# Filling products of identity and mask in any free bank of PSUM, in front of every operation of TensorE

## The chip, the cores and the metric

One core of one Trainium2 chip runs the kernel. Its engines are TensorE (PE, with its weight loads PEld), VectorE (DVE), ScalarE (ACT), GpSimd (POOL) and SyncE (SP, which here only issues DMAs). The metric is the device time of one execution in microseconds; of several runs the median is given.

## The reference

Attention with decay and without softmax (8 batches, 8 heads, 576 positions, 64 wide), then a mixture of experts with two of eight experts for each of 4608 tokens:

```python
scores = scale * np.matmul(q, k.transpose(0, 1, 3, 2))
Dmat = np.where(rel >= 0, gamma[:, None, None] ** rel[None, :, :], 0.0)
x = np.matmul(scores * Dmat[None], v)            # then (4608, 512)
noisy_logits = x @ w_gate + np.log1p(np.exp(x @ w_noise)) * noise
top2 = np.argpartition(-noisy_logits, 2, axis=1)[:, :2]
...
h = np.maximum(x[mask] @ w1[e], 0.0)             # 512 -> 1024
out[mask] += top2_w[mask, k, None] * (h @ w2[e]) # 1024 -> 512
```

## The kernel before

The attention is worked off in 16 units (a batch of a pair of batches and half of the heads, `u`), each with transposes of k and q (L558, L552), scores (L583), states (L616) and outputs (L651, L661). After each four units, which are one pair of batches, come a tail of 64 positions (L697 to L732), the routing logits (L769), the ranks of tokens (L832, L834), a table of places (L883) and the transposes of rows (L910) that are written to a table in HBM (`xd`). From that table the experts' tokens are gathered (L1026), transposed on TensorE (L1048) or by DMA, and go through the up products (L1103, or L1129 for the wide tiles) and the down products (L1191). Experts' tiles of the first three pairs of batches are worked off between units of attention; the rest follows.

What order the instructions have on each engine is decided when the program is built. All operations are recorded with a cost and a priority in a `Plan`; `Plan.run` then takes, one after another, the operation with the earliest planned start, reserves buffers for it, and keeps a planned clock for each engine (`free`). PSUM is a class "ps" of eight banks in `self.slots["ps"]`; an entry holds the planned time at which the bank comes free, its present user or `None`, and the tile. A bank has a user from the operation that opens it (which has it in `allocs`) until its last reader.

TensorE gets filling products: `warm` (L294) multiplies the identity with 256 columns of the attention's mask and writes the product, which nobody reads, to a bank. At L195 to L197 the planner notes how many of them go in front of an operation: only if that operation is on TensorE, has a planned start before `WARM` (170 us) and opens a bank. The count is 0.8 of the planned gap between the moment when TensorE and the operation's own bank are both free and its start, less 0.2 us, in products of 0.11 us. At L244 to L247, when all is planned, the operations are issued in their order, each behind its fillings. The planned times do not know of the fillings.

Which semaphores an instruction waits for follows from what it reads and writes: a filling that writes a bank waits until the bank's last reader is done, and on TensorE all that stands behind it waits with it.

Of the kernel before, what the change touches and what calls it, by code (L numbers as in the profile page):

```python
# [17 lines left out]
P = 128  # L18
# [36 lines left out]
class Plan:  # L55
# [23 lines left out]
    def op(self, eng, cost, fn, r=(), w=(), prio=0.0, dma=0, after=(), port=False, pace=0.0, slack=0.0, hold=0.0, late=0.0):  # L79
        o = Op()  # L80
        o.i, o.fn, o.prio, o.dma, o.port, o.pace, o.slack, o.hold = len(self.ops), fn, prio, dma, port, pace, slack, hold
        o.late, o.fill = late, 0
        o.eng = eng if isinstance(eng, dict) else {eng: cost}
        o.succ, o.allocs, o.bufs = [], [], []
        preds = set(after)
        for items, wr in ((r, False), (w, True)):
            for it in items:
                b, sub = it if isinstance(it, tuple) else (it, None)
                for s2, o2, w2 in b.acc:
                    if (wr or w2) and (sub is None or s2 is None or s2 == sub):  # L90
                        preds.add(o2)
                if b not in o.bufs:
                    o.bufs.append(b)
        for items, wr in ((r, False), (w, True)):
            for it in items:
                b, sub = it if isinstance(it, tuple) else (it, None)
                if wr:
                    b.acc = [a for a in b.acc if a[1] is o or not (sub is None or a[0] == sub)]
                b.acc.append((sub, o, wr))
        preds.discard(o)  # L100
        for b in o.bufs:
            if b.cls is not None:
                if not b.ops:
                    o.allocs.append(b)
                    self.fifo.setdefault((b.cls, b.stream), []).append(b)
                b.ops.append(o)
                b.left += 1
        o.preds, o.need = preds, len(preds)
        for p in preds:
            p.succ.append(o)  # L110
        self.ops.append(o)
        return o

    def run(self):
        free, dma_free, port, paced = {}, {}, [0.0], 0.0
# [34 lines left out]
        while ready:  # L150
            pick = None
            for o in ready:
                taken = []
                ok = all(b.cls is None or b.t is not None or b in o.allocs for b in o.bufs)
                if not ok:
                    continue
                for n, b in enumerate(o.allocs):
                    k = (b.cls, b.stream)
                    q = self.fifo[k]
                    m = len([t for t in taken if (t[1].cls, t[1].stream) == k])  # L160
                    if q[head[k] + m] is not b:
                        ok = False
                        break
                    x = slot(b, taken)
                    if x is None:
                        ok = False
                        break
                    taken.append((x, b))
                if not ok:
                    continue  # L170
                t0 = max([y[0] for x, b in taken for y in x], default=0.0)
                if o.pace:
                    t0 = max(t0, paced + o.pace)
                best = None
                for e, c in o.eng.items():
                    t = max(t0, free.get(e, 0.0))
                    if o.port and e in ("DVE", "POOL"):
                        t = max(t, port[0])
                    if o.dma and len(lanes[e]) >= 8:
                        t = max(t, lanes[e][-8].fin)  # L180
                    for p in o.preds:
                        t = max(t, p.fin + (o.hold + self.LAT if p.dma else 0.0 if p.on == e else self.LAT + o.late))
                    x = t + c + (self.BIAS.get(e, 0.0) if len(o.eng) > 1 else 0.0)
                    if best is None or x < best[0]:
                        best = x, e, t, c
                _, e, t, c = best
                key = (round(t * 20), o.prio, o.i)
                if pick is None or key < pick[0]:
                    pick = (key, o, e, t, c, taken)
            if pick is None:  # L190
                raise RuntimeError("no operation can go on: " + str([(o.i, o.prio) for o in ready[:20]]))
            _, o, e, t, c, taken = pick
            ready.remove(o)
            o.on = e
            if e == "PE" and t < self.WARM and o.allocs:  # L195
                x = max([free.get(e, 2.5)] + [y[0] for x, b in taken for y in x])
                o.fill = max(0, int((t - x - 0.2) * 0.8 / 0.11))  # L197
            free[e] = t + c
            if o.pace:
                paced = t  # L200
            if o.port and e in ("DVE", "POOL"):
                port[0] = t + c
            o.fin = t + c
            if o.dma:
                x = max(dma_free.get(e, 0.0), t + c)
                if e == "SP":
                    x += o.dma / 0.95
                else:
                    x += o.dma / 0.85
                    if dma_free.get("SP", 0.0) > t + c:  # L210
                        dma_free["SP"] += o.dma

                        for y in lanes["SP"][-8:] if o.dma > 2 else ():
                            if y.fin > t + c + self.DMA_LAT:
                                y.fin += o.dma
                dma_free[e] = x
                o.fin = dma_free[e] + self.DMA_LAT + o.slack
                lanes[e].append(o)
            for x, b in taken:
                for y in x:  # L220
                    y[1] = b
                b.t = x[0][2] if b.n == 1 else x[0][3]
                k = (b.cls, b.stream)
                head[k] += 1
                used[k] = used.get(k, 0) + b.n
            for b in o.bufs:
                if b.cls is None:
                    continue
                b.left -= 1
                if not b.left:  # L230
                    for x in self.slots[b.cls]:
                        if x[1] is b:
                            x[1] = None

                            x[0] = max(p.fin + (self.LAND if p.dma else 0.0) for p in b.ops) + self.LAT
                    used[(b.cls, b.stream)] -= b.n
            for s in o.succ:
                s.need -= 1
                if not s.need:
                    ready.append(s)  # L240
            order.append((o, t))
        assert len(order) == len(self.ops)
        self.log = [(t, o.on, o.fin, o.prio) for o, t in order]
        for o, t in order:  # L244
            if o.fill:
                self.warm([b for b in o.allocs if b.cls == "ps"][0], o.fill)
            o.fn(o.on)  # L247


class Kernel:  # L250
# [40 lines left out]
        else:  # L291
            self.eng(e).tensor_copy(out, in_)  # L292

    def warm(self, b, n):  # L294

        ident, mask = self.fixed["ident"].t, self.fixed["mask"].t
        for _ in range(n):
            self.nc.tensor.matmul(b.t[:, :2 * P], lhsT=ident, rhs=mask.rearrange("p r x -> p (r x)"), start=True, stop=True,  # L298
                                  skip_group_check=True)

    def psum(self, stream, n=1):
# [440 lines left out]
    def route(self, bp, prio):  # L742
# [56 lines left out]
        for j, op in ((0, Alu.max), (1, Alu.min)):  # L799
            o("DVE", DV, lambda e, j=j, op=op: V.tensor_tensor(kw(j), w1(), w2.t, op), ww, [at(("kw", j))])  # L800
# [12 lines left out]
        def s2(out, a, b, op, r, w):  # L813
            o("DVE", DV, lambda e: V.tensor_tensor(out(), a(), b(), op), r, w)
# [674 lines left out]
```

## Time and profile before

| | |
|---|---|
| time, median of 3 runs | 439.73 us (438.94 to 443.84) |
| the profiled execution | 438.11 us, span 436.6 us |
| TensorE busy | 386.1 us, 88% of the span, 4419 products |
| ScalarE, GpSimd, VectorE busy | 263.5, 288.1 and 154.4 us |
| mean granted clock of TensorE | 0.977 |
| moved by DMA | 95.92 MB, 220 GB/s in the mean |

A row of the profile's groups reads: line, engine, operation, what it writes and reads with buffer numbers left out, shapes and count; then busy time and mean ns of one; then the idle time of the engine ahead of these instructions, and what ended it. A row of the timeline has its start, the busy time, and in brackets the idle time ahead of it with what ended it; "issue" there means that the profile shows nothing that it waited for. A row of the stretches has busy times by engine, the clock that TensorE was granted (1.00 is full), the busy share of the DMA engines and GB/s.

### The profile page before, as it was taken

How to read it: one execution, taken by the hardware profiler on the slowest of the kernel's cores; microseconds unless marked ns; L12 is line 12 of the kernel's file. 1: busy time of each engine (PE TensorE's matmuls, PEld its weight loads, DVE VectorE, ACT ScalarE, POOL GpSimd, SP SyncE). 2: the span in 40 equal slices, each digit the busy share in tenths (PEclk: the TensorE clock that was granted, in tenths of full speed). 3: DMA queues.
4: the chain of work that ended last, by engine and by line, in shares of the span. 5: the costliest groups of instructions: out<-in, count | busy, mean ns of one | idle time of the engine just before them, and what ended most of it. 6: DMA issues, size and time to landing. Idle time of an engine off the chain costs nothing. (4 is left out here: it accounts for less than half of the span.)

```text
span 436.6 us, 11260 instructions
## 1 busy us (share of the span) xinstructions
PE 386.1 (88%) x4419; PEld 244.1 (56%) x4419; DVE 154.4 (35%) x455; ACT 263.5 (60%) x462; POOL 288.1 (66%) x315
## 2 busy tenths in 40 slices
PE   4987787876778999968999999999999999999992
PEld 3876576764566666725456654454454454454451
DVE  5654398696419979201034511103202100000001
ACT  2598687883668756433765755736647755555550
POOL 8755684681488836645367777776866878785583
PEclk9999698999899999989999999999999999999998
DMA  7996998999978999923249978999999969879395
GB/s 232 311 282 140 294 284 245 323 270 240 254 229 151 248 227 280 379 84 113 79 140 363 390 184 254 224 292 235 246 246 280 274 123 152 167 116 147 61 122 105
DMA packets 105177, 95.92 MB, mean 220 GB/s; under 512 B 42015, under 2 KB 82464, under 8 KB 105122
## 3 DMA queue, kind: packets, MB, share of 16 engines
q1 hardware_dynamic: 87298, 59.33, 48.4%
q0 software_dynamic: 17824, 35.85, 39.8%
q8 instruction: 35, 0.57, 0.6%
q14 instruction: 20, 0.16, 0.1%
HBM read 72.71 MB, written 26.36 MB: 227 GB/s over the span
## 5 line engine op out<-in xcount | busy, mean ns | idle before, releaser
L1191 PE MATMUL ps<-W,half 128*128 128x512 bf16 x576 | 189.7, 384 | 10.1 <-ACT half L1112 6.6
L1129 PE MATMUL ps<-big,W 128*128 128x512 bf16 (+4 forms) x640 | 182.4, 329 | 0.0
L1112 ACT ACTIVATE half<-ps 128x512 bf16<-128x512 f32 (+5 forms) x190 | 92.0, 503 | 102.3 <-PE ps L1129 59.4
L1235 POOL DMA_INDIRECT out_dram<-half,xg x74 | 96.9, 1309 | 51.6 <-issue 14.1
L1026 POOL DMA_INDIRECT xg<-xd,xi x80 | 82.8, 1036 | 50.0 <-issue 19.7
L1191 PEld LDWEIGHTS <-half 128*128 128x128 bf16 x576 | 55.0, 99 | 73.6 <-ACT half L1112 10.6
L1129 PEld LDWEIGHTS <-W 128*128 128x128 bf16 x640 | 62.5, 98 | 47.2 <-issue 1.0
L1229 ACT ACTIVATE half<-ps,xg 128x512 f32<-128x512 f32 (+1 forms) x57 | 38.5, 676 | 13.8 <-PE ps L1191 11.1
L591 DVE TENSOR_TENSOR half<-ps,mask 128x512 bf16<-128x512 f32 x64 | 40.3, 683 | 16.9 <-PE ps L583 12.8
L290 ACT ACTIVATE half<-ps 128x1024 bf16<-128x1024 bf16 (+1 forms) x38 | 37.0, 998 | 13.3 <-PE ps L558 6.0
L1231 DVE TENSOR_SCALAR half<-ps,xg 64x256 f32<-64x256 f32 (+1 forms) x22 | 13.2, 602 | 89.5 <-PE ps L1201 54.4
L1103 PE MATMUL ps<-half,W 128*128 128x256 bf16 (+1 forms) x288 | 29.3, 255 | 2.1 <-DMA W<-in_moe_w_dram 1.4
L298 PE MATMUL ps<-mask,ident__61 128*128 128x256 bf16 x147 | 21.9, 296 | 6.2 <-POOL mask L361 5.9
L1103 PEld LDWEIGHTS <-W 128*128 128x128 bf16 x288 | 23.9, 98 | 5.8 <-DMA W<-in_moe_w_dram 1.7
L292 DVE CAST W<-big 128x1024 bf16<-128x1024 f32 x18 | 12.0, 709 | 41.9 <-PE ps L1129 20.9
L290 ACT ACTIVATE tb<-ps 64x512 bf16<-64x512 f32 x32 | 18.8, 589 | 8.1 <-PE ps L616 3.7
L290 ACT ACTIVATE W<-big 128x1024 bf16<-128x1024 f32 x22 | 22.7, 1053 | 0.7 <-issue 0.5
L290 ACT ACTIVATE xT<-ps 128x512 bf16<-128x512 f32 (+1 forms) x39 | 19.6, 555 | 4.6 <-PE ps L661 1.8
L616 PE MATMUL ps<-half,half 64*64 64x64 bf16 (+2 forms) x512 | 18.2, 216 | 3.2 <-DVE half L591 1.4
L536 POOL TENSOR_TENSOR half<-big,tab 128x512 bf16<-128x512 f32 x16 | 16.6, 1050 | 5.8 <-DMA big<-in_v_dram 5.8
L529 POOL TENSOR_TENSOR half<-W,tabq 128x1024 bf16<-128x1024 f32 x6 | 11.4, 1901 | 13.1 <-DMA W<-in_q_dram 4.9
L298 PEld LDWEIGHTS <-ident__61 128*128 128x128 bf16 x147 | 14.5, 105 | 8.8 <-POOL ident__61 L353 4.6
(181 smaller groups left out, 436.5 us busy)
## 6 DMA issues: line engine op xcount, KB each, us to landing
big<-in_moe_w_dram SPq DMA_DIRECT2D x40, 512.0 KB
W<-in_moe_w_dram POOLq DMA_DIRECT2D x12, 512.0 KB
xd<-xg SPq DMA_DIRECT2D x16, 264.0 KB
W<-in_q_dram SPq DMA_DIRECT2D x16, 256.0 KB
big<-in_k_dram SPq DMA_DIRECT2D x8, 512.0 KB
big<-in_v_dram SPq DMA_DIRECT2D x8, 512.0 KB
big<-in_q_dram SPq DMA_DIRECT2D x16, 256.0 KB
W<-in_k_dram SPq DMA_DIRECT2D x6, 512.0 KB
```

The lines of the kernel that those rows point to most:

```text
L290: self.nc.scalar.activation(out, in_, Act.Copy)
L298: self.nc.tensor.matmul(b.t[:, :2 * P], lhsT=ident, rhs=mask.rearrange("p r x -> p (r x)"), start=True, stop=True, skip_group_check=True)
L536: self.eng(e).tensor_tensor(o, i, t, Alu.mult)
L591: nc.vector.tensor_tensor(S.t.bitcast(BF16).rearrange("p (h c x) -> p h c x", h=2, c=2)[:, h], p[h].t.rearrange("p (c x) -> p c x", c=2), ...
L616: nc.tensor.matmul(o[h * HD:(h + 1) * HD, hp, n, :], lhsT=kk[:k, r, c, y], rhs=vv[:k, r, c, y].unsqueeze(1).to_broadcast([k, n.stop - n.st ...
L1026: ins = nc.gpsimd.indirect_dma_start(out=x.t[:n, :], out_offset=None, in_=self.xd[:rows, :], in_offset=IOff(ap=xi.t[:n, h:h + 1], axis=0), ...
L1103: nc.tensor.matmul(pv()[:, f2, :], lhsT=w.t[:, o:o + P], rhs=xv()[:, di, :n], start=(di == 0), stop=(di == KD - 1))
L1112: self.nc.scalar.activation(o, i, Act.Relu)
L1129: self.mm = nc.tensor.matmul(p.t[:, :n], lhsT=w.t[:, o:o + P], rhs=xv()[:, di, :n], start=(di == 0), stop=(di == KD - 1))
L1191: self.mm = self.nc.tensor.matmul(po.t, lhsT=hv[:, c:c + P], rhs=self.W[e].t[:, o:o + DM], start=(f == 0), stop=(f == KF - 1))
L1229: nc.scalar.activation(y.t[:n, c], x, Act.Copy, scale=g()[:n])
L1235: ins = nc.gpsimd.indirect_dma_start(out=self.out[:, :], out_offset=IOff(ap=ix()[:n], axis=0), in_=y.t[:n, :], in_offset=None, bounds_chec ...
```

## The change

Fillings are now looked at for every operation of TensorE with a planned start before 170 us, whether it opens a bank or not. They go into the bank without a user that came free earliest, which may or may not be the one that the operation opens. The count comes from the planned gap between TensorE's and that bank's coming free and the operation's start. An operation carries the bank and the count (`o.fill`), and `warm` takes the bank's tile.

```diff
-        o.late, o.fill = late, 0
+        o.late, o.fill = late, None
...
-            if e == "PE" and t < self.WARM and o.allocs:
-                x = max([free.get(e, 2.5)] + [y[0] for x, b in taken for y in x])
-                o.fill = max(0, int((t - x - 0.2) * 0.8 / 0.11))
+            if e == "PE" and t < self.WARM:
+                b = min((x for x in self.slots["ps"] if x[1] is None), key=lambda x: x[0], default=None)
+                n = b and int((t - max(free.get(e, 2.5), b[0]) - 0.2) * 0.8 / 0.11)
+                if n and n > 0:
+                    o.fill = b[2], n
...
             if o.fill:
-                self.warm([b for b in o.allocs if b.cls == "ps"][0], o.fill)
+                self.warm(*o.fill)
...
-    def warm(self, b, n):
+    def warm(self, t, n):
...
-            self.nc.tensor.matmul(b.t[:, :2 * P], lhsT=ident, rhs=mask.rearrange("p r x -> p (r x)"), start=True, stop=True,
+            self.nc.tensor.matmul(t[:, :2 * P], lhsT=ident, rhs=mask[:, :2].rearrange("p r x -> p (r x)"), start=True, stop=True,
```

The mask's tile has two rows of 128, so `mask[:, :2]` is all of it. Two lines more stand in the new kernel from L200 on: L298 of before is L300 now, L651 is L653, and so on.

On TensorE, before, at the end of a unit's states (L616) and the start of the outputs of the unit ahead of it (L651), which the profile has at 74.0 us; `ps4_129` is bank 4 of PSUM, `half` are buffers in SBUF, and the brackets name the engine whose semaphore the row waits for:

```order
L616 LDWEIGHTS half16_98
L616 MATMUL ps0_125<-half19_101,half16_98 64x64
L651 LDWEIGHTS half1_83
L651 MATMUL ps4_129<-half13_95,half1_83 64x8x16 [waits Activation_49]
L651 LDWEIGHTS half1_83
L651 MATMUL ps1_126<-half13_95,half1_83 64x8x16 [waits Activation_49]
```

The same place on TensorE now:

```order
L618 LDWEIGHTS half16_98
L618 MATMUL ps0_125<-half19_101,half16_98 64x64
L300 LDWEIGHTS ident__61
L300 MATMUL ps4_129<-mask_143,ident__61 128x256 [waits Activation_49]
L300 LDWEIGHTS ident__61
L300 MATMUL ps4_129<-mask_143,ident__61 128x256
L300 LDWEIGHTS ident__61
L300 MATMUL ps4_129<-mask_143,ident__61 128x256
L653 LDWEIGHTS half1_83
L653 MATMUL ps4_129<-half13_95,half1_83 64x8x16
L653 LDWEIGHTS half1_83
L653 MATMUL ps1_126<-half13_95,half1_83 64x8x16 [waits Activation_49]
```

Three fillings stand in front of the outputs, in the bank that these open themselves, and the wait for ScalarE has moved from the first output product to the first filling.

On TensorE, before, between two gathered tiles of an expert (the two halves of the buffer `xg5`) that are transposed into one bank, at 86.8 us in the profile (`DMASW1` is the semaphore of the second tile's gather):

```order
L1048 LDWEIGHTS xg5_115
L1048 MATMUL ps0_125<-ident__61,xg5_115 128x128
L1048 LDWEIGHTS xg5_115 [waits DMASW1_49]
L1048 MATMUL ps0_125<-ident__61,xg5_115 128x128
L1048 LDWEIGHTS xg5_115
```

There now:

```order
L1050 LDWEIGHTS xg5_115
L1050 MATMUL ps0_125<-ident__61,xg5_115 128x128
L300 LDWEIGHTS ident__61
L300 MATMUL ps1_126<-mask_143,ident__61 128x256 [waits DVE_49]
L300 LDWEIGHTS ident__61
L300 MATMUL ps1_126<-mask_143,ident__61 128x256
L1050 LDWEIGHTS xg5_115 [waits DMASW1_49]
L1050 MATMUL ps0_125<-ident__61,xg5_115 128x128
```

Two fillings stand between the tiles, in another bank than that of the transposes, and the first of them waits for VectorE, which empties that bank.

## The prediction

> **What bounds the kernel now.** The page comes first: the span, and the row of its costliest groups that holds the filling products (mean in ns behind the busy time, then idle time before them).
>
> ```profile
> span 436.6 us, 11260 instructions
> L298 PE MATMUL ps<-mask,ident__61 128*128 128x256 bf16 x147 | 21.9, 296 | 6.2 <-POOL mask L361 5.9
> q8 instruction: 35, 0.57, 0.6%
> ```
>
> 147 products without a use take 21.9 us of TensorE. Whether time of TensorE is worth anything depends on the stage, so the second view is busy time by stretches: length, then busy us with counts for PE, PEld, DVE, ACT and POOL, granted clock, DMA share, GB/s.
>
> ```profile
> 40.00:80.00 40.00, 31.02 (x736) 26.70 (x737) 25.22 (x66) 29.01 (x48) 25.66 (x27) 0.87 0.95 269
> 80.00:120.00 40.00, 30.00 (x634) 23.85 (x631) 27.84 (x69) 26.60 (x45) 19.46 (x25) 0.96 1.05 267
> 120.00:160.00 40.00, 34.49 (x713) 26.97 (x711) 26.36 (x72) 29.96 (x52) 30.74 (x34) 1.00 0.95 214
> 212.00:430.00 218.00, 215.62 (x1288) 112.61 (x1285) 33.69 (x72) 125.92 (x231) 155.20 (x128) 1.00 0.90 207
> ```
>
> From 212 us on TensorE is busy 215.62 of 218 us at full clock: there it is the bound, and no filling stands there, before or now. In the attention stage, up to 160 us, it is busy 75 to 86% of each stretch, no engine is full, and the DMA share is 0.95 to 1.05: TensorE stands idle some 9 us of every 40 and waits for others, and the inputs arrive at the rate of the DMA. All that the change adds falls between 40 and 125 us, into this stage.
>
> The third view is the granted clock. The first dip in the trace begins at 47.56 us; stretches of 3.41 us laid from there show it whole or not at all (length, PE busy, clock, DMA share, GB/s).
>
> ```profile
> 44.15:47.56 3.41, 1.62 (x36) 1.00 0.99 282
> 47.56:50.97 3.41, 3.27 (x74) 0.50 1.07 320
> 50.97:54.39 3.42, 2.97 (x23) 0.50 1.09 308
> 68.04:71.46 3.42, 0.90 (x9) 1.00 0.80 210
> 71.46:74.87 3.41, 3.28 (x96) 0.50 0.92 259
> 105.59:109.00 3.41, 2.09 (x34) 1.00 0.85 236
> 109.00:112.42 3.42, 3.07 (x107) 1.00 0.70 190
> 112.42:115.83 3.41, 1.41 (x22) 1.00 0.94 256
> 115.83:119.24 3.41, 3.22 (x44) 0.50 1.05 296
> ```
>
> After a stretch with 1.62, 0.90 or 1.41 us of work the clock was 0.50; after one with 2.09 us it stayed 1.00. So in this run the line lies between 1.62 and 2.09 us of work in 3.41 us, and the fillings of before didn't keep TensorE above it at three places.
>
> **The change part by part.** The rule now looks at every operation of TensorE whose planned start is before 170 us, not only at those that open a bank, and puts the fillings into the free bank that came free first. The planned starts don't depend on fillings, so nothing else moves: the rows of DVE, ACT, POOL and SP stand as they stood, waits included, and the diff's slice of the mask is the same 256 columns. On TensorE, 20 groups with 147 products become 27 groups with 172. Seven groups are new, of 2, 5, 3, 2, 4, 3 and 5 products (24 in all); one group grows by one; one of four goes into another bank and loses a wait for ACT that ended nothing, since no idle time stood before it.
>
> Price of one product, from two groups of the old ones on the timeline (start, busy, idle before):
>
> ```profile
> 50.93 1.25 PE L298 MATMUL ps<-mask,ident__61 128*128 128x256 bf16 x5
> 83.76 1.05 PE L298 MATMUL ps<-mask,ident__61 128*128 128x256 bf16 x8
> ```
>
> Eight at full clock take 1.05 us, 0.13 each; five in the slow stretch 1.25, 0.25 each. All 25 are so worth 3.3 us at full clock and 6.3 at half. What counts is what stands behind each group. Here are the old rows around seven of the eight places, in order of time; in brackets the idle time before the row and what ended it.
>
> ```profile
> 40.86 0.55 PE L769 MATMUL ps<-wgn,xT 128*128 128x16 bf16 x16
> 42.14 0.32 PE L710 MATMUL ps<-half 64*64 64x64 bf16 x16 [0.26 <-ACT half L290]
> 45.94 0.62 PE L552 MATMUL ps<-ident__61,half 128*128 128x128 bf16 x8 [2.71 <-POOL half L529]
> 59.39 0.21 PE L651 MATMUL ps<-half,half 64*64 64x128 bf16 x1
> 60.24 0.64 PE L651 MATMUL ps<-half,half 64*64 64x128 bf16 x31 [0.63 <-DVE pay L814]
> 62.60 0.64 PE L583 MATMUL ps<-half,half 64*64 64x128 bf16 x32 [0.28 <-ACT half L290]
> 86.55 0.61 PE L1048 MATMUL ps<-ident__61,xg 128*128 128x128 bf16 x8
> 88.89 0.22 PE L832 MATMUL ps<-MM,ltri 128*128 128x144 bf16 x1 [1.73 <-DVE MM L805]
> 106.91 1.02 PE L1191 MATMUL ps<-W,half 128*128 128x512 bf16 x4 [2.13 <-DMA W<-in_moe_w_dram]
> 119.25 0.55 PE L769 MATMUL ps<-wgn,xT 128*128 128x16 bf16 x16
> 122.64 0.62 PE L697 MATMUL ps<-ident__61,half 128*128 128x128 bf16 x8 [1.06 <-POOL half L688]
> 124.38 0.32 PE L710 MATMUL ps<-half 64*64 64x64 bf16 x16 [0.67 <-ACT half L290]
> ```
>
> - Two in front of the routing logits (L769) at 40.9 us: 0.26 us. The next wait, 0.26 us for ACT's copy, ends when L697's result, which comes before the fillings, has been copied; so they use that wait up. Were they longer, 2.71 us for POOL stand behind. Cost 0.
> - Five in front of the first L651 at 59.4: 0.65 us against 0.63 us of waiting for DVE one product later. Cost 0.0.
> - One more in the group at 61.6: 0.13 against 0.28. Cost 0.
> - Two between the two gathered tiles that L1048 transposes at 86.8: 0.26 against 1.73 us of waiting for the routing's mask. Cost 0.
> - Four between the first down products (L1191) and those that wait for a weight: 0.52 against 2.13. Cost 0.
> - Three in front of the logits at 119.25: 0.39 against 1.06. Cost 0.
> - Five between the transposes of L1048 at 123.4: 0.65 against 0.67. Cost 0.
>
> The eighth place has no idle time behind it at once: three in front of L651 at 74.0.
>
> ```profile
> 72.40 1.68 PE L616 MATMUL ps<-half,half 64*64 64x64 bf16 x32
> 74.01 1.03 PE L651 MATMUL ps<-half,half 64*64 64x128 bf16 x32
> 77.73 0.32 PE L710 MATMUL ps<-half 64*64 64x64 bf16 x16 [0.33 <-ACT half L290]
> 78.36 0.63 ACT L520 ACTIVATE half<-W 128x512 bf16<-128x512 f32 x1 [0.69 <-DMA W<-in_k_dram]
> ```
>
> L616 runs into L651 there, in a slow stretch that ends at 74.87. The three cost up to 0.75 us; but L651, which took 1.03 us slow and takes 0.64 at full clock (the row at 60.24), moves out of the slow stretch by that and gives back up to 0.39. Some 0.36 us are left. They go through the work of L661, L883, L697 and L769 to L710, whose input ACT copies and which is then 0.36 us late itself. ACT has 0.69 us of waiting for a load of k ahead of it at 78.36, which takes the 0.36 up, so I put 0.0 to 0.1 us on the end; if that load came early, 0.4.
>
> The new waits: a filling waits until its bank has been read, and in TensorE's queue all stands behind it. At 59.4 and 74.0 the bank is the one that L651 itself opens, so the wait is the old one, earlier by no product. At 40.9, 86.8 and 119.2 it is a bank that DVE empties (L591), which TensorE wants later. The tightest is 86.8:
>
> ```profile
> 84.55 0.68 DVE L591 TENSOR_TENSOR half<-ps,mask 128x512 bf16<-128x512 f32 x1
> ```
>
> The last such reading ahead of it ends at 85.23, 1.6 us before the filling. Cost 0; if the reading were more than 1.6 us late, the transposes and then L832 would wait for it, but L832 waits 1.73 us longer for the same queue of DVE anyway.
>
> Sum: +0.0 to 0.1 us. The profiled execution took 438.11 us (436.6 of span and 1.5 around it), 1.6 below the median of 439.73; its sum is 438.2, and on the median's footing 439.8.
>
> **The rivals.**
>
> *Clock (faster).* More work in front of the weak stretches holds the clock up. The four slow windows above hold 3.27 + 2.97 + 3.28 + 3.22 = 12.7 us of work; at full clock it would take half, so at most 6.4 us go: 433.4. Against it: none of the new products falls into 44.15:47.56, 68.04:71.46 or 112.42:115.83, the stretches that bring the dips, and what is won there meets the waits listed above. For it: where such stretches begin may differ between executions, and then two products (0.26 us) can lift 1.62 to near the line. The Trainium skill ("TensorE: Matmul & The Clock Gate", Part 1) says that the clock halves after a whole idle window of about 3.4 us, and that the windows run freely. By that rule no dip could have come here, since the longest wait shown above is 2.71 us, and this rival would be worth nothing; the trace disagrees, with 1.62 us of work in the stretch ahead of a dip. That the windows shift between runs no run here shows yet. To pass 1%, three of the four windows must go and their gain must not be given back. Chance 0.16, of it 0.09 beyond 1%.
>
> *Fillings are paid (slower).* What TensorE waits for isn't fixed by the others but follows TensorE's own earlier work (L697 for L710, L583 for L591). Then each group pushes the next wait along instead of filling it, from 40.9 us on: 25 × 0.13 = 3.3 us gives 443.1, and at the slow clock's 0.25, 6.3 us gives 446.1. It passes 1% (4.4 us) only from 0.18 us a product, if most fall in slow stretches. Against it: five of the nine waits listed end on POOL, on DVE's routing chain or on a DMA. Chance 0.16, of it 0.11 beyond 1%.
>
> *Code moves.* 50 more instructions shift all that follows in the queue that brings code (q8 on the page). TensorE has waits that nothing explains:
>
> ```profile
> 116.02 0.98 PE L651 MATMUL ps<-half,half 64*64 64x128 bf16 x28 [1.18 <-issue]
> ```
>
> If these hang on where the code is cut, such a stop may go or come: 1.18 us, and with it the slow window behind it (half of 3.22), 2.8 us either way: 437.0 or 442.6. Nothing shows that it is so. Chance 0.08, within 1%.
>
> **How the numbers follow.** Forecast, all hidden, 0.60: 439.8. A measurement of this kernel, whose three runs spread from 438.94 to 443.84, tells about 1% from no change. Faster by over 1%: 0.09 (clock). Slower by over 1%: 0.11 (paid). Within: 0.60 + 0.07 + 0.05 + 0.08 = 0.80. The range takes in two slow windows gone (-3.2 us, 436.5) and all products paid at full clock (443.1), which leaves out 2 in 10.
>
> **What would show it.** Right: 172 products in the filling group, of about the same mean; the waits in front of L710 (124.4), L651 (60.2), L832 (88.9), L1191 (106.9) and L697 (122.6) shorter by what the fillings take, with the rows behind them starting at the same times; the stage from 212 us as long as before, and beginning within 0.5 us of the old time. Wrong: rows behind these places later by the fillings' length; idle time in front of a filling that ends on DVE or ACT; a different number of stretches at clock 0.50.

## The result

| | before | after |
|---|---|---|
| median | 438.99 us (433.29 to 443.84, 20 runs) | 437.56 us (435.13 to 446.41, 20 runs) |
| ratio after / before | | 1.0001, 95% interval 0.9978 to 1.0024 |
| profiled execution | 438.11 us, span 436.6 | 438.09 us, span 436.5 |
| mean granted clock in it | 0.977 | 0.968 |

The forecast was 439.8 us, no change, with a range of 436.5 to 443.1. The profile after, with the rows that answer to those of before: first the page's span and its row of the fillings (L300 now), and the queue that brings code.

```profile
span 436.5 us, 11310 instructions
L300 PE MATMUL ps<-mask,ident__61 128*128 128x256 bf16 x172 | 25.6, 291 | 6.2 <-POOL mask L363 5.9
q8 instruction: 35, 0.57, 0.6%
```

172 products: 3.7 us more in the row of the fillings, 5.2 us more of TensorE's busy time in all (391.3 against 386.1), and no more span. Where they went shows in the timeline of TensorE after, at the places that the prediction went through (start, busy, idle before with its releaser); lines of the kernel are two higher than before.

```profile
46.42 0.92 PE L554 MATMUL ps<-ident__61,half 128*128 128x128 bf16 x8
58.56 0.71 PE L300 MATMUL ps<-mask,ident__61 128*128 128x256 bf16 x5
59.20 0.68 PE L653 MATMUL ps<-half,half 64*64 64x128 bf16 x32
87.17 0.38 PE L300 MATMUL ps<-mask,ident__61 128*128 128x256 bf16 x2
87.83 0.22 PE L834 MATMUL ps<-MM,ltri 128*128 128x144 bf16 x1
104.22 0.60 PE L300 MATMUL ps<-mask,ident__61 128*128 128x256 bf16 x4
106.68 1.02 PE L1193 MATMUL ps<-W,half 128*128 128x512 bf16 x4 [1.85 <-DMA W<-in_moe_w_dram]
122.13 0.62 PE L699 MATMUL ps<-ident__61,half 128*128 128x128 bf16 x8 [0.73 <-POOL half L690]
123.86 0.32 PE L712 MATMUL ps<-half 64*64 64x64 bf16 x16
```

The waits of 0.63 us at 60, of 1.73 at 89 and of 0.67 at 124 are gone, those at 107 and 122 are 0.3 us shorter, and the rows behind start within 1.1 us of their old times. One wait is longer: that of L583 at 62.6 us, 0.28 us before, is 0.74 us now (L585 at 62.17). And the wait at 89 shrank by far more than the 0.26 us of its two fillings, with the row behind 1.06 us earlier. So two executions differ by more than a small group takes. From the first wide product on the two executions run side by side: 209.91 us before, 210.16 after.

The clock did not follow the fillings. Up to 212 us the execution after has seven stretches at clock 0.50, that of before five. Here are the stretches of 3.41 us ahead of six of the seven (length, PE busy, clock, DMA share, GB/s); each is followed by a stretch at 0.50:

```profile
40.25:43.66 3.41, 1.12 (x27) 1.00 0.67 173
67.56:70.97 3.41, 0.95 (x9) 1.00 0.88 201
88.04:91.45 3.41, 1.96 (x74) 1.00 1.09 271
111.93:115.34 3.41, 1.79 (x32) 1.00 0.88 269
129.00:132.41 3.41, 2.01 (x68) 1.00 0.98 226
204.09:207.50 3.41, 1.42 (x15) 1.00 0.55 195
```

### The profile page after: what moved, and what is told of

Its sections match the earlier page's. It is cut to its first block, busy times and chain, and to the rows that moved or that the text cites. A ratio compares the mean times of both kernels' runs of the same rounds, so it can differ in the third digit from the quotient of the medians.

```text
span 436.5 us, 11310 instructions
## 1 busy us (share of the span) xinstructions
PE 391.3 (90%) x4444; PEld 247.8 (57%) x4444; DVE 154.6 (35%) x455; ACT 264.7 (61%) x462; POOL 288.7 (66%) x315
## 5 line engine op out<-in xcount | busy, mean ns | idle before, releaser
L300 PE MATMUL ps<-mask,ident__61 128*128 128x256 bf16 x172 | 25.6, 291 | 6.2 <-POOL mask L363 5.9
L300 PEld LDWEIGHTS <-ident__61 128*128 128x128 bf16 x172 | 16.7, 104 | 9.7 <-POOL ident__61 L355 4.6
L618 PEld LDWEIGHTS <-half 128*64 128x64 bf16 (+1 forms) x512 | 15.3, 112 | 7.4 <-issue 4.6
```

The costliest lines, as they stand in the source:

```text
L300: self.nc.tensor.matmul(t[:, :2 * P], lhsT=ident, rhs=mask[:, :2].rearrange("p r x -> p (r x)"), start=True, stop=True, skip_group_check=True)
L618: nc.tensor.matmul(o[h * HD:(h + 1) * HD, hp, n, :], lhsT=kk[:k, r, c, y], rhs=vv[:k, r, c, y].unsqueeze(1).to_broadcast([k, n.stop - n.st ...
```

## The experiments

The chips on which they ran differ: the kernel before took 424.96 to 426.46 us in the median beside e1 to e11, and 441.76 beside e12. So each ratio is against the runs of before on the same chip. Cut lines of the edits are marked by three dots.

**Theories.** 1, hidden: the products lie in waits and the end doesn't see them. 2, paid and won back: each costs its time, and the clock gave it back. 3, the clock: what counts is how long TensorE is at half clock.

### e1_none: no fillings at all

```diff
         for o, t in order:
-            if o.fill:
-                self.warm(*o.fill)
             o.fn(o.on)
```

> The kernel after with no filling products at all (172 left out; the output does not depend on them). Theory 1, hidden: what TensorE does up to 125 us lies beside waits for others, so taking 172 products away (some 20 us of TensorE) moves the end by less than 1 us either way; the row of the fillings is gone and the idle time is longer by as much. Theory 2, paid and won back: each product costs its 0.11 us on the path, and the change came out at nothing only because the clock gave as much back; then the time falls by the products' cost less what the clock loses, several us in one direction. Theory 3, the clock: over the 20 runs of the kernel after, the time falls with the mean granted clock, about 0.3 us for each us less at half clock; without fillings there are more stretches at 0.50 (40 us or more in place of some 20), and the time rises by some 6 us, to about 444.

Measured: 428.15 us, ratio 1.0068 (1.0032 to 1.0104), mean clock 0.954 in its profile. From 40 to 80 us the clock fell to 0.74:

```profile
40.00:80.00 40.00, 29.98 (x682) 0.74 1.05 286
```

All fillings together are worth some 3 us (1.4 to 4.4 by the interval), much less than the 20 us of TensorE that they take and less than the 6 us that theory 3 asked for. Theory 1's "less than 1 us either way" fails, since the whole interval lies above it: the fillings as a whole aren't idle work, they win time. Theory 2's "several us in one direction" fits too. The 0.3 us per us at half clock that theory 3 started from hangs on two of the 20 runs (441.79 and 446.41 us); over the other 18 it is 0.13.

### e2_new_x4: the seven new groups four times as long

```diff
...
-                self.warm(*o.fill)
+                self.warm(o.fill[0], o.fill[1] * (4 if g in (11, 15, 18, 20, 22, 23, 25) else 1))
+                g += 1
```

> The kernel after with the seven new groups four times as long (96 products in place of 24: +72, 7.9 us at 0.11 each). Theory 1, hidden: the waits behind the groups take most of it; what is longer than its wait (59.4, 74.0, 119.2, 123.4 us) comes to some 4 us and is made up in later waits: 0 to +1.5 us at the end. Theory 2, paid: +7.9 us less what the clock gives, at least +4.

Measured: 426.47 us, ratio 1.0009 (0.9982 to 1.0036). Theory 1 holds and theory 2 falls for this dose: 72 products more did not show. In its timeline 12 products stand at 72.8 us in the place without a wait, and the row behind starts at 74.24, as it does after with three:

```profile
71.88 1.01 PE L620 MATMUL ps<-half,half 64*64 64x64 bf16 x32
72.82 1.49 PE L302 MATMUL ps<-mask,ident__61 128*128 128x256 bf16 x12
74.24 0.64 PE L655 MATMUL ps<-half,half 64*64 64x128 bf16 x32
```

In this execution the clock was full there: L616 (L620 here) took 1.01 us, and 1.68 in that of after. So part of the dose was given back by the clock, by chance of this execution.

### e3_late25 and e6_late100: the price where nothing hides it

One more group, of 25 or of 100 products, at the first operation of TensorE with a planned start of 260 us or later.

```diff
...
+            if e == "PE" and t >= 260.0 and not late:
+                late = 1
+                b = min((x for x in self.slots["ps"] if x[1] is None), key=lambda x: x[0])
+                o.fill = b[2], LATE
```

> The kernel after with 25 more products in one group at a planned start of 260 us, where TensorE is busy without a gap and the clock is full. All theories: nothing hides them there, the end moves by 25 x 0.11 = 2.8 us (+0.6%). It gives the price of the change's own count when it is paid in full, and shows whether so little can be told in this kernel.

Measured: 426.17 us, ratio 1.0008 (0.9980 to 1.0037). The +0.6% was not seen at the end. In the timeline the group takes its price, and the row behind starts 2.95 us after the group's start:

```profile
261.33 2.89 PE L306 MATMUL ps<-mask,ident__61 128*128 128x256 bf16 x25
264.28 0.38 PE L1199 MATMUL ps<-W,half 128*128 128x512 bf16 x1
```

The kernel after had not run on that chip, so its own footing was missing. Hence the next two, on another chip.

> The kernel after, unchanged, on the chip of the runs beside it, as their footing. All theories: the same as before within 0.3% (-1.3 to +1.3 us).

Measured (e5_again, the kernel after): 424.50 us, ratio 0.9980 (0.9947 to 1.0013).

> The kernel after with 100 more products in one group at a planned start of 260 us. If TensorE is the bound there, as its idle-free rows say: +11 us over the kernel after (100 x 0.11), with the rows behind the group later by 11 us up to the end. If the +0.3 us of the 25 is the true price (something else sets the pace there): +1 to +2 us, and idle time of TensorE behind the group gets shorter.

Measured: 434.87 us, ratio 1.0234 (1.0183 to 1.0284), 10.4 us above e5_again in the medians. Its timeline of TensorE:

```profile
265.20 0.38 PE L1199 MATMUL ps<-W,half 128*128 128x512 bf16 x1
265.42 11.08 PE L306 MATMUL ps<-mask,ident__61 128*128 128x256 bf16 x100
276.33 0.38 PE L1137 MATMUL ps<-big,W 128*128 128x512 bf16 x1
```

100 products push the next row by 10.9 us, and the end by 10.4 in the medians: 0.10 to 0.11 us each, paid in full. The 25 of e3 had the same price in their timeline; one comparison of this kernel doesn't tell 0.6% safely.

### e4_cover: long waits filled

73 products more, by the ordinal of the operation of TensorE.

```diff
+EXTRA = {41: 8, 46: 12, 77: 16, 128: 10, 148: 5, 284: 8, 285: 14}
...
+            more = EXTRA.get(npe - 1, 0) if e == "PE" else 0
...
+            if e == "PE" and (t < self.WARM or more):
...
+                n = (max(n, 0) if t < self.WARM else 0) + more if b else 0
...
```

> The kernel after with 73 more products put where the two profiles show long waits in front of or inside weak stretches: 8 in front of L697 at 40 us, 12 of L552 at 45, 16 of L583 at 70, 10 of L1191 at 106, 5 of L697 at 122, 8 and 14 of L1191 at 187 and 189. Theory 1, hidden: 0 within 1 us. Theory 2, paid: +8 us less the clock's part. Theory 3, the clock: three of the stretches at 0.50 go (at 44 to 48, 71 and 190 us), 10 us of slow clock at 0.3 are 3 us: -3 us.

Measured: 426.64 us, ratio 1.0023 (0.9992 to 1.0054), mean clock 0.994 in its profile, with no stretch at 0.50 before 420 us. The clock was held and nothing was won: theory 3 falls as it was put. So the fall of time with the clock over the runs of one kernel isn't shown to be a price of the clock; what the 73 products cost beside it, this run doesn't separate.

### e7_new_x10 and e8_one60: where the cover ends

The seven groups ten times as long (the edit of e2 with 10), and 60 products more at the one place without a wait (the edit of e4 with `EXTRA = {80: 60}`).

> The kernel after with the seven new groups ten times as long (240 products in place of 24: +216, 23.8 us). Theory 1, hidden: the waits behind the seven groups (1.2 + 0.6 + 0.3 + 1.7 + 2.1 + 1.1 + 0.7 us, and later ones in the stage) take a good part: +3 to +12 us. Theory 2, paid: +20 to +24 us.

Measured: 442.65 us, ratio 1.0423 (1.0377 to 1.0469), 18.2 us above e5_again for 23.8 us of products. This lies between both expectations: some 5.6 us were not paid, the rest was. How much of the 5.6 the waits hold and how much a fuller clock gave isn't separated.

> The kernel after with 60 products more in front of L651 at 74.0 us, the one place of the change without a wait behind it (63 in place of 3; 6.6 us). Theory 1, hidden: the stage has later waits for DVE, ACT and DMA of some 7 us in all up to 107 us that take it up: 0 to +1.5 us at the end, the rows at 107 us at their old times. Theory 2, paid: +6 us or more.

Measured: 432.98 us, ratio 1.0190 (1.0142 to 1.0237), 8.5 us above e5_again. Theory 1 as the prediction had it fails here. The timeline of TensorE in e5_again, from the fillings at 73.5 us to L712 (L710 of before):

```profile
73.51 0.82 PE L300 MATMUL ps<-mask,ident__61 128*128 128x256 bf16 x3
74.26 0.71 PE L653 MATMUL ps<-half,half 64*64 64x128 bf16 x32
77.62 0.32 PE L712 MATMUL ps<-half 64*64 64x64 bf16 x16 [0.33 <-ACT half L292]
```

The same rows in e8_one60:

```profile
74.57 7.84 PE L305 MATMUL ps<-mask,ident__61 128*128 128x256 bf16 x63
82.34 0.64 PE L658 MATMUL ps<-half,half 64*64 64x128 bf16 x32
85.63 0.32 PE L717 MATMUL ps<-half 64*64 64x64 bf16 x16 [0.33 <-ACT half L297]
```

All behind comes 8.0 us later (85.63 against 77.62; 1.06 us of it lie ahead of the fillings already, which start at 74.57 against 73.51), and the wait of 0.33 us for ACT is still there, to the hundredth. ACT's copy follows TensorE's work, so its wait moves along and takes nothing up. ACT itself waits for TensorE in this run:

```profile
83.41 1.08 ACT L297 ACTIVATE xT<-ps 128x512 bf16<-128x512 f32 x2 [7.54 <-PE ps L668]
```

The wait for a weight's load at 107 us, on which the prediction counted for another group, moves along too. GpSimd (POOL) issues these loads, and it waits itself for VectorE's routing, which is late as well. First the loads' issue and the row that waits in e5_again, then in e8_one60:

```profile
91.60 1.51 POOL L965 DMA_DIRECT2D W<-in_moe_w_dram  x2
106.97 1.02 PE L1193 MATMUL ps<-W,half 128*128 128x512 bf16 x4 [1.91 <-DMA W<-in_moe_w_dram]
```

```profile
99.31 0.46 POOL L850 TENSOR_TENSOR ub<-MM,bnd 128x144 f32<-128x144 bf16 x1 [7.31 <-DVE keep_w L815]
103.40 1.51 POOL L970 DMA_DIRECT2D W<-in_moe_w_dram  x2
118.54 1.02 PE L1198 MATMUL ps<-W,half 128*128 128x512 bf16 x4 [1.69 <-DMA W<-in_moe_w_dram]
```

The loads are issued 11.8 us later and the row starts 11.6 us later, so the delay of 8.0 us has grown on the way.

### e9_at70 and e10_at74: the same 24 products in two places

The edit of e4 with `EXTRA = {77: 24}`, and with `EXTRA = {80: 24}`.

> The kernel after with 24 products more, the change's own count, in front of L583 at 69 us (42 in place of 18), where TensorE waits some 2.5 us for ACT in every trace so far. Theory 1 as it stands now (a filling costs nothing only where the wait right behind it is longer; what is over that passes on to the end): 24 x 0.11 = 2.6 us against a wait of 2.2 to 2.7, so 0 to +0.4 us, and the wait in front of L583 is gone. Theory 2, paid wherever they stand: +2.6 us.

Measured: 423.89 us, ratio 0.9946 (0.9911 to 0.9981).

> The same 24 products more 3 us later, in front of L651 at 74 us (27 in place of 3), where no wait stands behind them. Theory 1 as it stands now: +2.6 us (0.6%) at the end, less up to 0.4 that the slow stretch gives back, and the wait of 0.33 us in front of L710 as long as before. The theory as the prediction had it (ACT's wait for a load and later waits take a delay up): 0 to +1 us.

Measured: 424.92 us, ratio 0.9986 (0.9954 to 1.0018). The difference of the two ratios is 0.4%, of the right sign; it is no more than the intervals allow for nothing. The +0.6% expected of e10 lies outside its interval against before. The timelines are clearer about the next rows. e9_at70:

```profile
67.44 4.75 PE L305 MATMUL ps<-mask,ident__61 128*128 128x256 bf16 x42
72.11 0.64 PE L590 MATMUL ps<-half,half 64*64 64x128 bf16 x32
73.95 0.64 PE L658 MATMUL ps<-half,half 64*64 64x128 bf16 x32
```

e10_at74:

```profile
71.64 0.65 PE L590 MATMUL ps<-half,half 64*64 64x128 bf16 x32 [2.56 <-ACT half L297]
73.43 4.33 PE L305 MATMUL ps<-mask,ident__61 128*128 128x256 bf16 x27
77.70 0.64 PE L658 MATMUL ps<-half,half 64*64 64x128 bf16 x32
```

In e9 the 24 have replaced the wait for ACT and L658 starts at 73.95; in e10 the wait of 2.56 us stands and L658 starts at 77.70, 3.4 us after its time in e5_again. At the first place they are hidden from TensorE's next row, at the second not. The delay is still there 40 us later, in L699 (L704 in e10). First e5_again, then e10_at74:

```profile
118.00 0.62 PE L699 MATMUL ps<-ident__61,half 128*128 128x128 bf16 x8 [0.43 <-POOL half L690]
```

```profile
121.89 0.62 PE L704 MATMUL ps<-ident__61,half 128*128 128x128 bf16 x8 [0.43 <-POOL half L695]
```

These are two executions on two chips: the same row starts at 117.48, 119.51 and 120.23 us in those of e3, e6 and e9, which have no more products than the change at 74 us, so the delay by then is 1.7 to 4.4 us. At the first wide product it can't be told any more: 198.82 us in e10, 193.89 to 200.09 in the executions of e1 to e4 on the same chip. That execution of e10 took 427.29 us, that of e5_again 422.23, but over all runs e10's median is only 0.4 us above e5_again's. The traces show the delay, the times don't show its price at the end.

### e11_warm75: no fillings after 75 us

```diff
-    WARM = 170.0
+    WARM = 75.0
```

> The kernel after with fillings only up to a planned start of 75 us (37 of the 172 left out), since traces so far pass a delay on from there. Theory 1 as it stands now: the groups at 83.6 and 94 us have little wait behind them, so up to 1.3 us are won, -0.3%; the clock: one or two more stretches at 0.50 between 75 and 130 us cost up to 1.7 us each. Within 0.3% of the kernel after, either way.

Measured: 425.97 us, ratio 1.0016 (0.9985 to 1.0046). Nothing that can be told, as expected.

### e12_old70: is the 0.5% of e9 real?

```diff
...
-                o.fill = max(0, int((t - x - 0.2) * 0.8 / 0.11))
+                o.fill = max(0, int((t - x - 0.2) * 0.8 / 0.11)) + (24 if npe == 78 else 0)
```

> The kernel before, with its old rule for fillings, and 24 products more in front of L583 at 70 us (42 in place of 18): the change's count in one place that has a wait. If the 0.5% of e9_at70 against before come from that place (the wait filled, and no slow stretch at 71 us behind it: L583 and L616 at full clock, 1.1 us), then -0.3 to -0.5% here too, without the change's seven groups. If they were scatter: within 0.2% of before.

Measured: 441.41 us, ratio 0.9991 (0.9954 to 1.0027). In its timeline the wait in front of L583 is gone too and L583 and L616 run at full clock:

```profile
66.13 4.75 PE L300 MATMUL ps<-mask,ident__61 128*128 128x256 bf16 x42
70.81 0.65 PE L585 MATMUL ps<-half,half 64*64 64x128 bf16 x32
71.28 0.99 PE L618 MATMUL ps<-half,half 64*64 64x64 bf16 x32
```

The place does what was expected, and no gain follows that can be told from nothing. e9 stays the only version whose interval lies below before; against the kernel after, which ran on another chip, its lead is 0.3% with intervals that overlap. That a version beats both is not shown.

## Why the prediction was right, and where its reasons were not

**The count and the order.** 172 products, and as many instructions on every other engine as before (455, 462 and 315 on VectorE, ScalarE and GpSimd): as predicted. The prediction's 0.13 us a product was a little too dear, against 0.11 in e6: a group's last product is counted with its whole length, which weighs more in 8 products (1.05 us) than in 100 (11.08 us).

**Seven places with a wait right behind.** Right for all of them together: the five waits named as signs are gone or shorter (above), and four times the products (e2) did not show. For each place by itself the two traces don't prove it, since waits changed by up to 1.5 us more than the fillings take, in both directions. e7 shows that the cover ends: with ten times the products most of them are paid.

**The eighth place, 74.0 us.** The size was right and the reason wrong. The row L661 stood at 74.97 us before, 3.38 us behind L583 (71.59); after it stands at 74.86, 3.79 us behind L583 (71.07): 0.41 us for an estimate of 0.36. But the step "ACT has 0.69 us of waiting for a load, which takes the 0.36 up" failed. In the execution after, ACT doesn't wait for that load at all, which is the case for which the prediction itself named 0.4 us:

```profile
77.42 0.62 ACT L522 ACTIVATE half<-W 128x512 bf16<-128x512 f32 x1
```

And the 0.36 us pass on: counted from L583, L710 comes 6.14 us later before and 6.50 after. e8 shows the same with a large dose: ACT and the wait in front of L710 follow TensorE. So no wait close behind takes the 0.36 us up; whether the end sees them can't be told, since they are 0.1%, and e10's seven times as much didn't show in the times either. The ratio's interval is 1 us wide to either side, so the forecast's 0.0 to 0.1 us is not told from 0.4.

**"Whether time of TensorE is worth anything depends on the stage."** The premise that the attention stage runs at the rate of the DMA, up to 160 us, was too wide. A delay of TensorE at 74 us passes to the end when it is large (e8: 8.5 us for 6.6 us of products). There the loads themselves came later, since GpSimd issued them later. For a delay as large as that of all new products together this stays open: e10's 24 products (2.6 us, some 0.6%) delay all rows up to 122 us, and its ratio of 0.9986 (0.9954 to 1.0018) doesn't show it. Busy shares of 75 to 86% with a full DMA do not show that an engine has time in hand.

**The rival "fillings are paid".** At e6's price the 25 products ask for 2.7 us, at the prediction's for 3.3. The ratio of 1.0001 (0.9978 to 1.0024) leaves 1 us at most, so they are not paid in full. Nor did the clock pay for them: the profiled execution after had seven stretches at 0.50 in place of five, and over the runs beside e5_again the mean clock was 0.982 after and 0.980 before.

**The clock rival.** Its bound, one line between 1.62 and 2.09 us of work in 3.41 us, did not hold. The prediction shows some of the stretches only. With stretches laid over all of both executions, in steps of 3.41 us from the dips, some with less work than 2.01 us are followed by full clock. First one of after, then one of before, each with the stretch behind it:

```profile
33.42:36.83 3.41, 1.70 (x47) 1.00 0.71 91
36.83:40.25 3.42, 2.96 (x111) 1.00 0.68 150
```

```profile
129.48:132.89 3.41, 1.98 (x71) 1.00 0.86 208
132.89:136.30 3.41, 3.41 (x65) 1.00 1.18 194
```

The stretches at 105.10 us after (1.83 us of work) and at 204.57 us before (1.81) are followed by full clock too. So in the execution after the clock was kept after 1.70 and 1.83 us of work and halved after 1.79, 1.96 and 2.01: between 1.7 and 2.0 us TensorE's busy time alone doesn't decide it, and what does is open. Nor does the bound say why the second stretch of the first dip (50.97:54.39) was slow, with 3.27 us of work ahead of it. The prediction's sign "a different number of stretches at clock 0.50" came true, seven for five, and the time stayed. That the stretches begin elsewhere in another execution is now seen: the first dips begin at 47.56 and 43.66 us, which differ by 3.90 us and not by a multiple of 3.41. In e4, without any dip up to 420 us, the time is the same. Why a full clock brought nothing there, while no fillings at all cost 0.7%, is not settled; e4's own products may have cost what the clock gave.

**Code moves.** The stop at 113 to 116 us stands in the execution after at 113 to 115.5, though 34 instructions more lie ahead of it (17 products with their loads). In e5_again, the same kernel, the stop isn't there at all. So it doesn't hang on where the code is cut alone; on what it hangs is open. First the execution after, then e5_again:

```profile
115.48 0.96 PE L653 MATMUL ps<-half,half 64*64 64x128 bf16 x26 [0.49 <-issue]
```

```profile
112.81 0.64 PE L653 MATMUL ps<-half,half 64*64 64x128 bf16 x32
```

## What to carry to other kernels

Work without a use is surely hidden only where the wait right behind it is longer, and up to that length; go through the places one by one and don't count on later waits, since a wait for an engine that is fed by the delayed one moves along with it, and so can a wait for a load that such an engine issues (e8). Small excesses may still be lost on the way (e2, e10); these runs don't show where. Whether a wait follows can be tested with one run: put a large dose in front of it, and see in the trace whether the wait is still there, to the hundredth. Price such work first where nothing can hide it, with a dose well above the scatter: 100 products gave 0.11 us each, 25 gave no answer.

## What the runs showed of the hardware that was not expected

The dips of TensorE's clock last one or two stretches of 3.41 us and, within one execution, begin at whole multiples of 3.41 us from each other (47.56, 71.46, 115.83 and 190.92 us before). The clock was halved after stretches in which TensorE had worked up to 2.01 us, so a dip doesn't take a long idle gap; but it was also kept after 1.70, 1.81, 1.83 and 1.98 us, so no one line in the busy time parts the two. And the same kernel, before, ran between 424.96 us and 441.76 us in the median on different chips, 4%, with 1.4 to 3.1% between the shortest and the longest run beside each group of experiments.
